# A gated linear-attention and MLP kernel, planned in source, against a written-out order in which two pairs hold neighbouring tokens together

## The chip, the cores and the metric

The kernel runs on one core of a Trainium2 chip. The metric is the time of one execution in microseconds (us) on the device, the median of several runs; lower is better. The core has five engines with queues of their own that run in order: TensorE (PE, matmuls, with weight loads shown as PEld), VectorE (DVE), ScalarE (ACT), GpSimd (POOL) and SyncE (SP, which here only issues DMAs). Where a DMA is issued from SP or POOL, it is moved by DMA engines that all queues share.

## The reference

```
f = 1 / (1 + exp(-f_logit))                        # q, k, v, f_logit: (4, 8, 768, 48) float32
for t in range(768):                               # state: 48 x 48 per batch and head
    state = f[t][:, None] * state + outer(k[t], v[t])
    y[t] = q[t] @ state
x = y as (4 * 768, 8 * 48)                         # 3072 tokens of 384
h = x @ w_in                                       # w_in (384, 2048)
out = (h * sigmoid(h)) @ w_out                     # w_out (2048, 384)
```

## The kernel before, in words

A unit is one chunk of 128 tokens of one batch with all 8 heads; there are 6 chunks x 4 batches = 24 units, and two neighbouring units (two batches of one chunk) make a pair, 12 in all. Within a unit the recurrence is done in chunk form. E and L (ScalarE) make log(1 + exp(-f_logit)). cs (PE) sums it along the tokens with a triangular matrix and gives the chunk's total with a matmul by ones. ia, a and al (ScalarE) are exponentials of those sums. ki and qg multiply them on k and q; vb casts v. tq (PE) transposes both products, eight 128x128 pieces per unit, and qkc copies them out of PSUM. sc (PE) makes the scores, at (VectorE) masks them, y (PE) multiplies by v and adds q times the state. yc casts y, yT (PE) transposes it, xc copies it to xT. d, sd and su carry the state to the next chunk of the batch. The MLP takes a pair at a time: mi (PE) makes 2 of 16 blocks of the hidden layer, six matmuls of 256 columns; si (ScalarE) applies silu; mo (PE) is a quarter of the second product for one unit, four matmuls of 384 columns; oc copies and so stores. wi and wo are four loads each of the two weights, cast to bf16 by POOL's DMA queue.

Every step is a task with an engine, a planned duration and buffers of fixed counts (SLOTS). `schedule` simulates the five queues with rank numbers from CFG, and the program emits the tasks by planned start. So the order of each engine is fixed when the program is built, and on the chip each engine waits for the next instruction of that order. PSUM's eight banks are dedicated: three to the MLP (`mlp`), two to the scores, one each to tq with yT, to cs, and to y with d. The loads take 192-byte runs, one token of one head each; the first two pairs are loaded unit by unit (192 KB per DMA), the others by pair (384 KB). An exponential table that has both exp and ln is loaded once ahead; the later table loads are put in by the compiler ahead of the activations that need one.

Of the kernel before, what the change touches and what calls it, by code (L numbers as in the profile page):

```python
# [37 lines left out]

SLOTS = dict(f=5, k=6, q=6, v=5, e=2, lf=3, ia=2, qk=5, vb=6, qkT=4, atm=3, yb=3, xT=4, hT=4, sd=2, al=6, o=3,
             st0=1, st1=1, st2=1, st3=1, mlp=3, sc=1, tq=1, cs=1, yd=1)  # L40

LAT = {"PE": 0.25, "ACT": 0.14, "DVE": 0.14, "POOL": 0.08, "SP": 0.0}
TABLE = 1.29


class Task:
    def __init__(self, name, eng, dur, prio, deps=(), acq=(), use=(), mode=None, phase=None, load=0.0):
        self.name, self.eng, self.dur, self.prio = name, eng, dur, prio
        self.deps, self.acq, self.use = list(deps), list(acq), list(use)
        self.mode, self.phase, self.load = mode, phase, load  # L50


class Inst:
    def __init__(self, key, cls):
        self.key, self.cls = key, cls


def make_tasks(cfg):
    T, tasks, pace, R = {}, [], cfg["pace"], cfg["rank"]

    def add(name, *a, **k):
        t = Task(name, *a, **k)
        T[name] = t
        tasks.append(t)
        return t

    kb = lambda n: n * 1024.0 / (cfg["dma_rate"] * 1e3)
    I = {}

    def inst(key, cls):  # L70
        if key not in I:
            I[key] = Inst(key, cls)
        return I[key]

    base = lambda u: pace * u
    for P in range(PAIRS):
        u0 = 2 * P
        for n, x in enumerate("fkqv"):
            inst((x, P), x)
        groups = [(u0,), (u0 + 1,)] if P < 2 else [(u0, u0 + 1)]  # L80
        for us in groups:
            for n, x in enumerate("fkqv"):
                add((x, us), "SP", 0.35 * len(us), base(us[0]) + R['ld'] + n * 0.1, acq=[I[x, P]], load=kb(192 * len(us)))
    load_of = lambda x, u: T[x, (u,)] if u < 4 else T[x, (u - u % 2, u - u % 2 + 1)]

    for P in range(PAIRS):
        us_list = [(2 * P,), (2 * P + 1,)] if P < 2 else [(2 * P, 2 * P + 1)]
        for us in us_list:
            n = len(us)
            ph = us[0] // 2 - 1 if us[0] >= 4 else 0  # L90
            e = add(("E", us), "ACT", 0.067 + 0.32 * n, base(us[0]) + R['E'], deps=[T["f", us]], acq=[inst(("e", us), "e")],
                    use=[I["f", P]], mode="exp", phase=ph)
            add(("L", us), "ACT", 0.067 + 0.32 * n, base(us[0]) + R['E'] + 0.1, deps=[e], acq=[inst(("lf", P), "lf")],
                use=[I["e", us]], mode="exp", phase=ph)
    log_of = lambda u: T["L", (u,)] if u < 4 else T["L", (u - u % 2, u - u % 2 + 1)]

    for u in range(UNITS):
        c, b, P, B = u // BATCHES, u % BATCHES, u // 2, base(u)
        last, ph = c == CHUNKS - 1, u // 2
        dmat = u >= cfg["turned"]  # L100
        for key in ("cs", "ia", "qk", "vb", "qkT", "atm", "yb", "sc", "al"):
            inst((key, u), key)
        inst(("y", u), "yd"), inst(("d", u), "yd"), inst(("tq", u), "tq"), inst(("yT", u), "tq")
        inst(("sd", u), "sd"), inst(("st", u), f"st{b}"), inst(("xT", P), "xT"), inst(("hT", P), "hT")
        cs = add(("cs", u), "PE", 0.162 + (0 if last else 0.1), B + R["cs"], deps=[log_of(u)], acq=[I["cs", u]], use=[I["lf", P]])
        ia = add(("ia", u), "ACT", 0.387, B + R["ia"], deps=[cs], acq=[I["ia", u]], use=[I["cs", u]], mode="exp", phase=ph)
        a = add(("a", u), "ACT", 0.38, B + R["ia"] + 0.1, deps=[ia], use=[I["cs", u]], mode="exp", phase=ph)
        if not last:
            al = add(("al", u), "ACT", 0.19, B + R["ia"] + 0.2, deps=[cs], acq=[I["al", u]], use=[I["cs", u]], mode="exp", phase=ph)
        ki = add(("ki", u), "POOL", 1.02, B + R["ki"], deps=[ia, load_of("k", u)], acq=[I["qk", u]], use=[I["ia", u], I["k", P]])  # L110
        vb = add(("vb", u), "POOL", 0.62, B + R["vb"], deps=[load_of("v", u)], acq=[I["vb", u]], use=[I["v", P]])
        qg = add(("qg", u), "DVE", 0.45, B + R["qg"], deps=[a, load_of("q", u)], acq=[I["qk", u]], use=[I["cs", u], I["q", P]])
        if dmat:
            qkT = add(("qkD", u), "SP", 2.3, B + R["tq"], deps=[qg, ki], acq=[I["qkT", u]], use=[I["qk", u]], load=0.5)
        else:
            tq = add(("tq", u), "PE", 0.45, B + R["tq"], deps=[qg, ki], acq=[I["tq", u]], use=[I["qk", u]])
            qkT = add(("qkc", u), "DVE", 0.6, B + R["qkc"], deps=[tq], acq=[I["qkT", u]], use=[I["tq", u]])
        sc = add(("sc", u), "PE", 0.41, B + R["sc"], deps=[qkT], acq=[I["sc", u]], use=[I["qkT", u]])
        at = add(("at", u), "DVE", 1.21, B + R["at"], deps=[sc], acq=[I["atm", u]], use=[I["sc", u]])
        yd = [at, vb] + ([T["su", u - BATCHES]] if c else [])  # L120
        y = add(("y", u), "PE", 0.39 if c else 0.22, B + R["y"], deps=yd, acq=[I["y", u]],
                use=[I["atm", u], I["vb", u], I["qkT", u]] + ([I["st", u - BATCHES]] if c else []))
        yc = add(("yc", u), "DVE", 0.47, B + R["yc"], deps=[y], acq=[I["yb", u]], use=[I["y", u]])
        yT = add(("yT", u), "PE", 0.17, B + R["yT"], deps=[yc], acq=[I["yT", u]], use=[I["yb", u]])
        xc = add(("xc", u), "DVE", 0.3, B + R["xc"], deps=[yT], acq=[I["xT", P]], use=[I["yT", u]])
        if not last:
            d = add(("d", u), "PE", 0.17, B + R["d"], deps=[ki, vb, y], acq=[I["d", u]], use=[I["qk", u], I["vb", u]])
            sdd = [d] + ([T["su", u - BATCHES]] if c else [])
            sd = add(("sd", u), "DVE", 0.47, B + R["sd"], deps=sdd, acq=[I["sd", u]],
                     use=[I["d", u]] + ([I["st", u - BATCHES]] if c else []))  # L130
            add(("su", u), "POOL", 0.75, B + R["su"], deps=[sd, al], acq=[I["st", u]], use=[I["sd", u], I["al", u]])

    for n in range(4):
        add(("wi", n), "POOL", 0.8, R["wi"] + n, deps=[T["ki", cfg["w_after"][n]]], load=786.432e3 / 341e3)
    for n in range(4):
        add(("wo", n), "POOL", 0.8, R["wo"] + n, deps=[T["ki", cfg["w_after"][4 + n]]], load=786.432e3 / 341e3)

    for P in range(PAIRS):
        B = base(2 * P + 1)
        for j in range(NTILES // 2):  # L140
            h = inst(("h", P, j), "mlp")
            mi = add(("mi", P, j), "PE", 0.655, B + R["mi"] + j * R["mstep"], deps=[T["xc", 2 * P], T["xc", 2 * P + 1], T["wi", j // 2]],
                     acq=[h], use=[I["xT", P]])
            add(("si", P, j), "ACT", 0.504, B + R["si"] + j * R["mstep"], deps=[mi], acq=[I["hT", P]], use=[h], mode="silu")
        for i in range(2):
            u = 2 * P + i
            o = inst(("o", u), "mlp")
            for m in range(4):
                mo = add(("mo", u, m), "PE", 0.655, B + R["mo"] + (4 * i + m) * R["mstep"],
                         deps=[T["si", P, 2 * m], T["si", P, 2 * m + 1], T["wo", m]] + ([T["mo", u, m - 1]] if m else []),  # L150
                         acq=[o], use=[I["hT", P]])
# [405 lines left out]
```

## Time and profile before

| | us |
|---|---|
| median of 3 timed runs | 221.58 (218.91 to 223.65) |
| span of the profiled execution (the results list no other time for it) | 217.2 |
| busy, PE / DVE / ACT / POOL | 181.0 / 102.7 / 149.4 / 75.0 |

The profile is one execution, from its first to its last instruction; the timed runs have launch and end around that. Busy time counts the time in which an instruction of the engine was under way, and matmuls overlap one another.

### The profile page before, as it was taken

What the parts mean: (1) busy time and instruction counts of PE and PEld (TensorE: products, weight loads), DVE (VectorE), ACT (ScalarE), POOL (GpSimd) and SP (SyncE); (2) the same over time, 40 slices, a digit from 0 to 9 for tenths busy, and PEclk for the clock granted to TensorE, in tenths of its full rate; (3) what the DMA queues carried; (4) which work ended last, traced back from release to release, by engine and by line L of the source; (5) the groups of instructions that cost most, each with busy time, mean ns of one, the idle gap of its engine ahead of it and who ended that gap; (6) DMA issues with size and microseconds to landing.
All of it is one profiled execution on the core that took longest, in us unless ns stands there. A gap on an engine that the chain in (4) does not pass through costs nothing.

```text
span 217.2 us, 4591 instructions
## 1 busy us (share of the span) xinstructions
PE 181.0 (83%) x1872; PEld 135.4 (62%) x1872; DVE 102.7 (47%) x201; ACT 149.4 (69%) x230; POOL 75.0 (35%) x126
## 2 busy tenths in 40 slices
PE   0366889945999966969969969986999999999992
PEld 0344668624578646648748738754769677786761
DVE  3277730027455526545545446444585573745111
ACT  4444249965079899995999995999845658662440
POOL 2248830042274146144343335235253321510100
PEclk9999999995699999999999999999999999999999
DMA  7999999999999999999999999011001010100101
GB/s 121 164 163 169 196 188 184 178 164 187 174 223 220 164 200 167 197 194 177 179 194 180 163 191 185 4 38 38 3 36 39 0 39 36 39 36 3 41 31 72
DMA packets 104628, 27.02 MB, mean 124 GB/s; under 512 B 99712, under 2 KB 103552, under 8 KB 104608
## 3 DMA queue, kind: packets, MB, share of 16 engines
q1 hardware_dynamic: 99488, 19.27, 70.1%
q0 software_dynamic: 5120, 7.47, 15.1%
q8 instruction: 14, 0.23, 0.5%
q14 instruction: 6, 0.05, 0.1%
HBM read 25.17 MB, written 4.72 MB: 138 GB/s over the span
## 4 chain that ended last, share of the span: by engine, by line
PE 62%; ACT 19%; DMA 6%; SPq 5%; issue 3%; DVE 2%; POOL 0%; DVEq 0%; ACTq 0%; POOLq 0%
PE mlp L412 27%; PE mlp L422 21%; SPq L381 5%; ACT L438 4%; DMA w_out_sb<-in_moe_w_out_dram 3%; PE tq L454 3%; ACT lf L390 3%; PE sc L465 3%; ACT L390 3%; DMA f<-in_f_logit_dram 2%; ACT e L388 2%; ACT L388 2%; ACT ia L438 2%; PE yd L478 2%; PE cs L431 2%
## 5 line engine op out<-in xcount | busy, mean ns | idle before, releaser
L408 ACT ACTIVATE hT<-mlp 128x512 bf16<-128x512 f32 x96 | 56.1, 597 | 28.6 <-PE mlp L412 25.0
L422 PE MATMUL mlp<-w_out_sb,hT 128*128 128x384 bf16 x384 | 71.5, 331 | 2.6 <-DMA w_out_sb<-in_moe_w_out_dram 2.6
L412 PE MATMUL mlp<-xT,w_in_sb 128*128 128x256 bf16 x576 | 68.8, 276 | 3.3 <-DVE o L425 1.7
L412 PEld LDWEIGHTS <-w_in_sb 128*128 128x128 bf16 x576 | 55.8, 99 | 11.5 <-issue 3.6
L422 PEld LDWEIGHTS <-hT 128*128 128x128 bf16 x384 | 35.6, 99 | 23.0 <-issue 3.6
L469 DVE TENSOR_TENSOR atm<-sc,triu 128x512 bf16<-128x512 f32 x48 | 30.9, 685 | 31.0 <-PE sc L465 30.9
L444 POOL TENSOR_TENSOR qk<-k,ia 128x384 bf16<-128x384 f32 x24 | 23.9, 996 | 58.5 <-ACT ia L438 50.4
L448 DVE TENSOR_TENSOR qk<-q,cs 128x384 bf16<-128x384 f32 x24 | 13.2, 550 | 37.5 <-ACT al L442 36.3
L428 POOL DMA_DIRECT2D out_dram<-o x22 | 12.7, 576 | 41.6 <-DVE o L425 36.7
L505 POOL TENSOR_TENSOR st<-sd,al 48x192 bf16<-48x192 f32 x40 | 20.0, 500 | 19.4 <-DVE sd L499 8.2
L438 ACT ACT_TABLE_LOAD x14 | 18.0, 1283 | 9.2 <-PE cs L435 8.6
L454 PE MATMUL tq<-ident,qk 128*128 128x128 bf16 x192 | 16.8, 238 | 8.9 <-DVE xT L488 6.2
L456 DVE COPY qkT<-tq 128x1024 bf16<-128x1024 bf16 x24 | 16.5, 687 | 8.5 <-PE tq L454 8.5
L425 DVE COPY o<-mlp 128x384 f32<-128x384 f32 x24 | 13.2, 552 | 15.0 <-PE mlp L422 14.9
L454 PEld LDWEIGHTS <-qk 128*128 128x128 bf16 x192 | 13.2, 106 | 11.2 <-issue 6.9
L438 ACT ACTIVATE ia<-cs 128x384 f32<-128x384 f32 x24 | 11.7, 490 | 11.6 <-PE cs L435 7.5
L431 PE MATMUL cs<-lf,triu 128*128 128x384 bf16 x24 | 8.4, 350 | 13.2 <-ACT lf L390 7.9
L482 DVE CAST yb<-yd 128x384 bf16<-128x384 f32 x24 | 13.3, 554 | 10.9 <-PE yd L478 10.7
L388 ACT ACTIVATE e<-f 128x768 f32<-128x768 f32 (+1 forms) x14 | 10.5, 748 | 8.0 <-DMA f<-in_f_logit_dram 8.0
L446 POOL CAST vb<-v 128x384 bf16<-128x384 f32 x24 | 11.7, 503 | 10.5 <-issue 5.0
L435 PEld LDWEIGHTS <-lf 128*128 128x128 bf16 x80 | 5.1, 100 | 15.1 <-issue 13.8
L408 ACT ACT_TABLE_LOAD x10 | 12.8, 1283 | 0.2
(35 smaller groups left out, 154.3 us busy)
## 6 DMA issues: line engine op xcount, KB each, us to landing
out_dram<-o POOLq DMA_DIRECT2D x22, 192.0 KB, 3.9
f<-in_f_logit_dram SPq DMA_DIRECT2D x10, 384.0 KB, 8.1
k<-in_k_dram SPq DMA_DIRECT2D x10, 384.0 KB, 7.7
q<-in_q_dram SPq DMA_DIRECT2D x10, 384.0 KB, 7.9
v<-in_v_dram SPq DMA_DIRECT2D x10, 384.0 KB, 7.8
w_in_sb<-in_moe_w_in_dram POOLq DMA_DIRECT2D x4, 384.0 KB, 9.2
w_out_sb<-in_moe_w_out_dram POOLq DMA_DIRECT2D x4, 384.0 KB, 12.0
f<-in_f_logit_dram SPq DMA_DIRECT2D x4, 192.0 KB, 5.2
```

Of the source, the lines that this page charges most:

```text
L388: nc.scalar.activation(e, at("f", u // 2)[:, i:i + n, :, 0:D], AF.Exp, scale=-1.0)
L408: return nc.scalar.activation(at("hT", P)[:, 2 * j:2 * j + 2, :], h, AF.Silu)
L412: nc.tensor.matmul(h[:, i, :], w_in_sb[:, kk, n * 128:(n + 1) * 128], at("xT", P)[:, kk, :], start=(kk == 0), stop=(kk == KT - 1))
L422: nc.tensor.matmul(o, at("hT", P)[:, n, i * C:(i + 1) * C], w_out_sb[:, n, :], start=(n == 0), stop=(n == NT - 1))
L425: nc.vector.tensor_copy(at("ob", u), at("o", u)[:, 0:d_model])
L438: nc.scalar.activation(at("ia", u).rearrange("p h d -> p (h d)"), at("cs", u)[:, 0:HD], AF.Exp)
L444: nc.gpsimd.tensor_mul(at("qk", u)[:, 1, :, 0:D], at("k", P)[:, i, :, 0:D], at("ia", u))
L454: nc.tensor.transpose(t_ps[:, j, p, :], at("qk", u)[:, j, 2 * p:2 * p + 2, :], ident)
L456: nc.vector.tensor_copy(at("qkT", u), at("tq", u).rearrange("p (j n c) -> p j n c", j=2, c=C))
L469: nc.vector.tensor_mul(at("atm", u)[:, r], at("sc", u)[:, r], triu[:, None, :].to_broadcast([C, NP, C]))
L482: nc.vector.tensor_copy(at("yb", u), at("y", u))
L505: nc.gpsimd.tensor_mul(at("st", u)[lo:lo + D, :, r * D:(r + 1) * D], at("sd", u)[lo:lo + D, :, r * D:(r + 1) * D], at("al", u)[lo:lo + D, ...
```

## The change

The planner is gone: the order of all engines, the engine of each step and its buffers are now written out in a string, PLAN, of `name.pair.index:engine:buffer`, with P, A, V, G and S for PE, ACT, DVE, POOL and SP. PAIRS says which (batch, chunk) units a pair holds. Pairs 0 and 1 are of form T: chunks 0 and 1 of batch 0, and of batch 1. In a T pair partition p holds tokens 2p and 2p + 1, so that the loads take runs of 384 bytes; index 0 or 1 is then the even or the odd token in cs, ia, ki, tq, sc and at, while y, d and what follows are again by chunk (rows 0 to 63 and 64 to 127). Pairs 2 to 11 are of form N, two batches of one chunk as before. yc, oc, vb, qkc, xc and sd may run on ScalarE now, ki and qg on VectorE or POOL. All PSUM tiles come from one pool of eight banks, pb. For pairs 0 and 1, mi is done in halves of 128 columns, one unit each. From pair 6 on, tq with qkc is replaced by a DMA transpose, qkD, and yT with xc by yD, both in SP's queue. `idle` is a number of matmuls on zeros. The k, q and v loads of N pairs go unit by unit, f by pair. Table loads are issued by the program at each turn between the exponentials and silu.

```diff
+PAIRS = [
+    ('T', (0, 0), (0, 1)),
+    ('T', (1, 0), (1, 1)),
+    ('N', (2, 0), (3, 0)),
...
+PLAN = """
+f.0.0:S:0 f.0.1:S: f.1.0:S:1 k.0.0:S:0 q.0.0:S:0 E.0.0:A:0 q.1.0:S:1 E.0.1:A: L.0.1:A:0 k.1.0:S:1 L.0.0:A: E.1.0:A:1 idle.512.17::7 cs.0.0:P:0
...
-    tasks = planned(CFG, SLOTS)
...
+            if T:
+                h = H // parts
+                w = h * 2 * D
+                src = SRC[kind][b, j * h:(j + 1) * h, c * C:(c + 2) * C].rearrange("h (p t) d -> p h (t d)", t=2)
+                dst = at(kind, P)[:, j * w:(j + 1) * w].rearrange("p (h w) -> p h w", h=h)
...
+                cols = slice(rest[2] * C, (rest[2] + 1) * C) if len(rest) > 2 else slice(0, 2 * C)
                 for kk in range(KT):
-                    nc.tensor.matmul(h[:, i, :], w_in_sb[:, kk, n * 128:(n + 1) * 128], at("xT", P)[:, kk, :],
+                    nc.tensor.matmul(h[:, i, cols], w_in_sb[:, kk, n * 128:(n + 1) * 128], at("xT", P)[:, kk, cols],
                                      start=(kk == 0), stop=(kk == KT - 1))
...
+        if kind == "y" and T:
+            first = [True, True]
+            for j in range(2):
+                for h in range(H):
+                    for r in range(2):
+                        rows = slice(r * HC, (r + 1) * HC)
+                        nc.tensor.matmul(at("y", P, r)[:, D * h:D * (h + 1)], at("atm", P, j)[rows, h % 2, h // 2, :],
+                                         at("vb", P, j)[rows, h, :], start=first[r], stop=(j == 1), skip_group_check=True)
...
         elif kind == "oc":
-            nc.vector.tensor_copy(at("ob", u), at("o", u)[:, 0:d_model])
+            copy(eng, at("ob", P, i), at("o", P, i)[:, 0:d_model])
...
+            if T:
+                for j in range(2):
+                    nc.tensor.matmul(main, tincl if j <= i else tstrict, lf[:, j, :, 0:D], start=(j == 0), stop=(j == 1), skip_group_check=True)
...
         elif kind == "qkD":
-            nc.sync.dma_start_transpose(out=at("qkT", u).rearrange("p j n c -> p (j n) c"),
-                                        in_=at("qk", u).rearrange("p j h d -> p (j h d)"))
+            nc.sync.dma_start_transpose(out=at("qkT", P, i).rearrange("p j n c -> p (j n) c"), in_=at("qk", P, i).rearrange("p j h d -> p (j h d)"))
...
+        elif kind == "yD":
+            nc.sync.dma_start_transpose(out=at("xT", P)[:, :, i * C:(i + 1) * C], in_=at("yb", P, i))
...
+    def run(kind, rest, eng, got):
+        if kind == "idle":
+            for _ in range(rest[1]):
+                nc.tensor.matmul(buf["pb", int(got)][:, 0:rest[0]], triu, zero[:, 0:rest[0]], start=True, stop=True, skip_group_check=True)
+            return
...
+    modes = [(n, mode_of(kind)) for n, (kind, *_) in enumerate(plan) if mode_of(kind)]
+    turns = {n: TABLES[m2] for (n, m), (_, m2) in zip(modes, modes[1:]) if m != m2}
...
+        for n, t in enumerate(plan):
+            if t not in loads:
+                run(*t)
+            if n in turns:
+                nc.scalar.preload_act_table_set(turns[n])
```

ScalarE, before, the exponentials of the third pair (f2, lf2; one cs bank) after the silu of the first two:

```order
L388 ACT_TABLE_LOAD
L388 ACTIVATE e0_83<-f2_63 128x768
L390 ACT_TABLE_LOAD
L390 ACTIVATE lf2_87<-e0_83 128x16x48
L438 ACT_TABLE_LOAD
L438 ACTIVATE ia0_88<-cs0_139 128x384
L440 ACTIVATE cs0_139<-cs0_139 128x384
L442 ACTIVATE al4_125<-cs0_139 128x4
L438 ACTIVATE ia1_89<-cs0_139 128x384
```

And now, the turn ahead of the exponentials of pair 3 (f3), with a copy of xT among them:

```order
L478 ACT_TABLE_LOAD
L232 ACTIVATE e1_84<-f3_64 128x768
L239 ACTIVATE lf0_85<-e1_84 128x16x48
L312 ACTIVATE al4_132<-pb2_142 128x4
L183 COPY xT2_120<-pb1_141 128x3x128
L312 ACTIVATE al5_133<-pb6_146 128x4
L310 ACTIVATE x2_90<-pb6_146 128x384
L310 ACTIVATE x3_91<-pb6_146 128x384
L310 ACTIVATE x4_92<-pb2_142 128x384
L310 ACTIVATE x1_89<-pb2_142 128x384
```

The table load behind E and the one ahead of ia are gone; one stands at the turn. In all, ScalarE's queue has 38 table loads before and 20 now.

POOL, before, from the first w_in loads to the last w_out load (st is su's result, qk4 is ki of the third pair's first unit):

```order
L400 DMA w_in_sb_144<-in_moe_w_in_dram 128x3x512 x3
L444 TENSOR_TENSOR qk3_93<-k1_67,ia1_89 128x8x48
L505 TENSOR_TENSOR st10_131<-sd1_120,al1_122 48x4x48 x2
L400 DMA w_in_sb_144<-in_moe_w_in_dram 128x3x512
L446 CAST vb3_98<-v1_79 128x384
L403 DMA w_out_sb_145<-in_moe_w_out_dram 128x4x384 x3
L505 TENSOR_TENSOR st20_132<-sd0_119,al2_123 48x4x48 x2
L505 TENSOR_TENSOR st30_133<-sd1_120,al3_124 48x4x48 x2
L444 TENSOR_TENSOR qk4_94<-k2_68,ia0_88 128x8x48
L403 DMA w_out_sb_145<-in_moe_w_out_dram 128x4x384
```

And now, what follows on one row with all four w_in loads and two casts of v (st00 and st10 are su of the T pairs, qk4 and qk1 are qg of pair 2, st30 and st20 su of its units):

```order
L386 TENSOR_TENSOR st00_148<-sd0_126,al1_129 48x4x48 x2
L386 TENSOR_TENSOR st10_149<-sd1_127,al0_128 48x4x48 x2
L386 TENSOR_TENSOR st10_149<-sd0_126,al0_128 48x4x48 x2
L386 TENSOR_TENSOR st00_148<-sd1_127,al1_129 48x4x48 x2
L208 DMA w_out_sb_162<-in_moe_w_out_dram 128x4x384
L315 TENSOR_TENSOR qk4_97<-q2_73,x4_92 128x8x48
L315 TENSOR_TENSOR qk1_94<-q2_73,x1_89 128x8x48
L208 DMA w_out_sb_162<-in_moe_w_out_dram 128x4x384
L386 TENSOR_TENSOR st30_151<-sd0_126,al3_131 48x4x48 x2
L208 DMA w_out_sb_162<-in_moe_w_out_dram 128x4x384 x2
L386 TENSOR_TENSOR st20_150<-sd1_127,al2_130 48x4x48 x2
```

The w_out loads stand behind su of the T pairs, qg and su of pair 2.

SP, before, loads of pairs (number after the letter: buffer):

```order
L381 DMA f1_62<-in_f_logit_dram 128x16x48
L381 DMA k0_66<-in_k_dram 128x16x48
L381 DMA q0_72<-in_q_dram 128x16x48
L381 DMA v1_79<-in_v_dram 128x16x48
L381 DMA f2_63<-in_f_logit_dram 128x16x48
```

And now, in the place of pairs 6 and 7:

```order
L226 DMA v1_78<-in_v_dram 128x8x48
L226 DMA k1_66<-in_k_dram 128x8x48
L330 DMA_TRANSPOSE qkT1_106<-qk3_96 128x8x128
L226 DMA f0_61<-in_f_logit_dram 128x16x48
L226 DMA v0_77<-in_v_dram 128x8x48
L226 DMA k2_67<-in_k_dram 128x8x48
L226 DMA k1_66<-in_k_dram 128x8x48
L330 DMA_TRANSPOSE qkT3_108<-qk1_94 128x8x128
L371 DMA_TRANSPOSE xT2_120<-yb0_115 128x3x128
L226 DMA f1_62<-in_f_logit_dram 128x16x48
L371 DMA_TRANSPOSE xT2_120<-yb1_116 128x3x128
L330 DMA_TRANSPOSE qkT2_107<-qk4_97 128x8x128
```

Loads stand between transposes, each of which waits for its input.

## Rows read from the trace of the kernel before

**Rows 1.** The page: busy share of each engine, and GB/s in 40 slices.

```profile
PE 181.0 (83%) x1872; PEld 135.4 (62%) x1872; DVE 102.7 (47%) x201; ACT 149.4 (69%) x230; POOL 75.0 (35%) x126
...
GB/s 121 164 163 169 196 188 184 178 164 187 174 223 220 164 200 167 197 194 177 179 194 180 163 191 185 4 38 38 3 36 39 0 39 36 39 36 3 41 31 72
```

**Rows 2.** Stretches: from:to, length, busy (count) per engine, PEclk, DMA share, GB/s.

```profile
24.35:62.30 37.95, 31.22 (x266) 22.50 (x265) 12.70 (x24) 22.37 (x34) 10.06 (x16) 0.87 1.31 186
62.30:150.00 87.70, 75.15 (x841) 57.06 (x840) 44.53 (x85) 79.62 (x115) 36.08 (x62) 1.00 1.13 160
150.00:213.46 63.46, 62.92 (x647) 47.40 (x646) 31.11 (x58) 36.46 (x60) 16.52 (x26) 1.00 0.08 29
```

**Rows 3.** The chain: start, us, piece; attention and MLP pieces of TensorE.

```profile
62.31 0.26 PE cs L431
...
65.08 0.33 PE sc L465 x8
...
65.69 0.45 PE tq L454 x8
66.14 3.29 PE mlp L412 x30
...
137.63 0.28 PE yd L474 x4
137.91 0.20 PE yd L478 x8
138.10 1.95 PE mlp L422 x12
...
142.14 0.20 PE yd L494 x4
```

**Rows 4.** The chain: w_out, and ScalarE from 72 to 147 us.

```profile
47.11 7.54 DMA w_out_sb<-in_moe_w_out_dram
...
72.22 1.28 ACT L390
...
93.04 0.84 ACT lf L390
93.90 1.28 ACT L438
95.20 0.49 ACT ia L438
...
146.35 1.28 ACT L390
```

**Rows 5.** Timeline of the first 25 us: start, us, engine, instruction [idle before].

```profile
3.96 0.52 ACT L388 ACTIVATE e<-f 128x384 f32<-128x384 f32 x1 [1.95 <-DMA f<-in_f_logit_dram]
...
16.70 1.14 SPq L381 DMA_DIRECT2D v<-in_v_dram  x1
...
23.29 11.42 SPq L381 DMA_DIRECT2D q<-in_q_dram  x1
...
24.35 1.46 PE L412 MATMUL mlp<-xT,w_in_sb 128*128 128x256 bf16 x6
```

**Rows 6.** DMA: two queues (packets, MB, share of 16 engines), and issues with KB each and us to landing.

```profile
q1 hardware_dynamic: 99488, 19.27, 70.1%
q0 software_dynamic: 5120, 7.47, 15.1%
...
q<-in_q_dram SPq DMA_DIRECT2D x10, 384.0 KB, 7.9
...
f<-in_f_logit_dram SPq DMA_DIRECT2D x4, 192.0 KB, 5.2
```

**Rows 7.** Groups by line: name, count | busy us, mean ns | idle before.

```profile
L469 DVE TENSOR_TENSOR atm<-sc,triu 128x512 bf16<-128x512 f32 x48 | 30.9, 685 | 31.0 <-PE sc L465 30.9
...
L448 DVE TENSOR_TENSOR qk<-q,cs 128x384 bf16<-128x384 f32 x24 | 13.2, 550 | 37.5 <-ACT al L442 36.3 <-ACT cs L440 1.2
...
L438 ACT ACTIVATE ia<-cs 128x384 f32<-128x384 f32 x24 | 11.7, 490 | 11.6 <-PE cs L435 7.5 <-PE cs L431 4.0
```

More of the change, by code (lines that the diff above doesn't have):

```diff
@@ L39 @@
[L39 to L50, printed above, removed]
@@ L53 @@
[L53 to L151, printed above, removed]
-            oc = add(("oc", u), "DVE", 0.47, B + R["oc"] + 4 * i, deps=[mo], acq=[inst(("ob", u), "o")], use=[o])
-            late = u >= UNITS - 2
-            add(("so", u), "SP" if late else "POOL", 0.35 if late else 0.8, B + R["so"] + 4 * i, deps=[oc], use=[I["ob", u]],
-                load=0.6)
-    return tasks, T
@@ L320 @@
+mo.11.0.3:P: oc.11.0:A:5 so.11.0:S:
+"""
 @with_exitstack
@@ L363 @@
     ones = sb.tile([C, 1], BF16, name="ones")
+    zero = sb.tile([C, 512], BF16, name="zero")
+    two = any(kind == "T" for kind, *_ in PAIRS)
+    if two:
+        tincl = sb.tile([C, C], BF16, name="tincl")
+        tstrict = sb.tile([C, C], BF16, name="tstrict")
+        halves = sb.tile([C, 2], BF16, name="halves")
+        masks = [sb.tile([C, C], BF16, name=f"mask{j}") for j in range(2)]
     w_in_sb = sb.tile([128, KT, d_ff], BF16, name="w_in_sb")
@@ L371 @@
+    where_u = {(b, c): (P, i) for P, (kind, *us) in enumerate(PAIRS) for i, (b, c) in enumerate(us)}
     where = {}
[L372 to L374 removed]
     at = lambda *key: where[key]
[L377 to L381 removed]
@@ new lines, in emit @@
+        if kind == "d" and T:
+            todo = [r for r in range(2) if us[r][1] < CHUNKS - 1]
+            for j in range(2):
+                vv = at("vb", P, j).rearrange("p (n r) d -> p n (r d)", r=2)
+                for p in range(NP):
+                    for r in todo:
+                        rows = slice(r * HC, (r + 1) * HC)
+                        d_ps = at("d", P, r)[:, 0:HD].rearrange("p (n w) -> p n w", w=2 * D)
+                        nc.tensor.matmul(d_ps[:, p, :], at("qk", P, j)[rows, 1, 2 * p:2 * p + 2, :], vv[rows, p, :],
+                                         start=(j == 0 and p == 0), stop=(j == 1), skip_group_check=True)
+            return
@@ L476, in emit @@
                     first = False
-            for h in range(H):
-                nc.tensor.matmul(y[:, D * h:D * (h + 1)], at("atm", u)[:, h % 2, h // 2, :], at("vb", u)[:, h, :],
-                                 start=first, stop=True, skip_group_check=True)
-                first = False
+            if kind == "y":
+                for h in range(H):
+                    nc.tensor.matmul(y[:, D * h:D * (h + 1)], at("atm", P, i)[:, h % 2, h // 2, :], at("vb", P, i)[:, h, :],
+                                     start=first, stop=True, skip_group_check=True)
+                    first = False
@@ L508, in emit, with takes @@
         else:
             raise ValueError(kind)
+    def takes(kind, rest):
+        if kind in ("wi", "wo", "so", "yi", "idle"):
+            return []
+        P = rest[0]
+        T = PAIRS[P][0] == "T"
+        if kind in SRC:
+            return [(kind, P)]
+        if kind in ("E", "L"):
+            return [("e" if kind == "E" else "lf", P)]
+        if kind == "mi":
+            return [("h", P, rest[1])]
+        if kind in ("si", "xc", "yD"):
+            return [("hT" if kind == "si" else "xT", P)]
+        if kind == "al":
+            return [("al", *rest)]
+        if T and kind in ("y", "d"):
+            return [(kind, P, i) for i in range(2) if kind == "y" or PAIRS[P][1 + i][1] < CHUNKS - 1]
+        if kind in ("qkc", "qkD"):
+            return [("qkT", P)] if T else [("qkT", *rest)]
+        if kind == "sc":
+            return [(f"s{r}", *rest) for r in range(2)]
+        if kind == "at":
+            return [("atm", *rest[:2])]
+        if kind == "mo":
+            return [("o", *rest[:2])]
+        return [({"ki": "qk", "qg": "qk", "yc": "yb", "oc": "ob", "su": "st"}.get(kind, kind), *rest[:2])]
@@ new lines @@
+    cls_of = lambda kind: {"e": "e", "ia": "x", "a": "x", "cs": "pb", "tq": "pb", "y": "pb", "yT": "pb", "d": "pb", "o": "pb", "s0": "pb",
+                           "s1": "pb", "h": "pb"}.get(kind, kind)
+    mode_of = lambda kind: "silu" if kind == "si" else "exp" if kind in ("E", "L", "ia", "a", "al") else None
+    TABLES = {"exp": "natural_log_exp_and_others", "silu": "silu_and_others"}
+    def run(kind, rest, eng, got):
+        if kind == "idle":
+            for _ in range(rest[1]):
+                nc.tensor.matmul(buf["pb", int(got)][:, 0:rest[0]], triu, zero[:, 0:rest[0]], start=True, stop=True, skip_group_check=True)
+            return
+        slots = iter(got.split(",") if got else [])
+        for key in takes(kind, rest):
+            if key not in where:
+                cls = cls_of(key[0])
+                if cls == "st":
+                    cls = f"st{PAIRS[key[1]][1 + key[2]][0]}"
+                elif cls == "qkT" and len(key) == 2:
+                    cls = "qkTT"
+                where[key] = buf[cls, int(next(slots))]
+        assert next(slots, None) is None, (kind, rest, got)
+        emit(kind, rest, eng)
@@ L516 @@
         make_upper_triangular(nc, triu, 1.0, diag=True)
+        nc.vector.memset(zero, 0.0)
         nc.vector.memset(ones, 1.0)
+        if two:
+            nc.gpsimd.memset(tincl, 0.0)
+            nc.gpsimd.memset(tstrict, 0.0)
+            for r in range(2):
+                half = slice(r * HC, (r + 1) * HC)
+                make_upper_triangular(nc, tincl[half, half], 1.0, diag=True)
+                make_upper_triangular(nc, tstrict[half, half], 1.0, diag=False)
+            nc.vector.memset(halves, 0.0)
+            for r in range(2):
+                nc.vector.memset(halves[r * HC:(r + 1) * HC, r:r + 1], 1.0)
@@ L523 @@
             nc.vector.memset(buf[f"st{b}", 0], 0.0)
-        for t in tasks:
-            if t not in first:
-                emit(t)
+        if two:
+            for r in range(2):
+                half = slice(r * HC, (r + 1) * HC)
+                for j in range(2):
+                    for t in range(2):
+                        nc.vector.tensor_copy(masks[j][half, t * HC:(t + 1) * HC], (tincl if j <= t else tstrict)[half, half])
+        for n, t in enumerate(plan):
+            if t not in loads:
+                run(*t)
+            if n in turns:
+                nc.scalar.preload_act_table_set(turns[n])
 _INS = ['q', 'k', 'v', 'f_logit', 'moe_w_in', 'moe_w_out']
```

488 lines of the change are left out of this document (225 added, 263 removed).

## Prediction

> **What bounds the kernel now.** I read the busy shares first, then stretches of the span, the chain that ended last, and single rows. TensorE is the busiest engine and ScalarE the next [rows 1]. The stretches say where TensorE loses time [rows 2]. Up to 24.35 us it mostly waits for the first loads and the attention steps of the first units. From 24.35, where the first MLP matmul runs, to 62.3 it is busy 31.22 of 37.95 us, at a granted clock of 0.87 on average. From 62.3 to 150 it is idle for 87.70 - 75.15 = 12.55 us, and ScalarE is busy 79.62 of the 87.70. From 150 on it is idle for half a microsecond; then 3.74 us (217.20 - 213.46) of last copy and store follow.
>
> Busy time overstates overlapping matmuls, so I price PE work by chain pieces, where one piece begins as the other ends [rows 3]: six 256-column matmuls (one mi) 3.29 / 30 x 6 = 0.66 us, four 384-column ones (one mo) 0.65, the eight transposes of tq 0.45 (three, yT: 0.17), sc 0.33, the state part of y 0.28, its other part 0.20, d 0.20, cs 0.26. All of before: 96 mi 63.2, 96 mo 62.4, tq 10.8, yT 4.1, sc 7.9, y 24 x 0.20 + 20 x 0.28 = 10.4, d 4.0, cs 6.2: 169.0 us. Ahead of 24.35 lie four cs, tq and sc, three y, two yT and d, 5.5 us. So 163.5 us of work take 213.46 - 24.35 = 189.1 us, and **25.6 us are lost**: 13.1 after 62.3 (12.55 + 0.54), 12.5 before. The 12.5 hang on the fourth w_out load: it stands in POOL's queue behind the ki of the third pair, is issued at 47.11 and lands 7.54 us later [rows 4], and the matmuls after it run at the lower level for some time.
>
> **PE work.** The change takes 12 of 24 tq and 12 of 24 yT off PE (units of pairs 6 to 11): 12 x 0.62 = 7.4 us less. It adds in the first two pairs, by matmul counts at the same prices: sc 16 instead of 8 matmuls, 4 x 0.33 = 1.3; y and yi 0.8; d 0.8; cs 0.7. The mi in halves has twice the matmuls of half the columns; tq's row (128 columns, 0.056 us each) puts that at no cost. New total 165.2. Ahead of the first mi now stand nearly all attention of the T pairs and cs of pair 2: cs 2.2, tq 1.8, sc 2.6, d 1.6, y and yi 1.9, yT 0.3 = 10.4. **Left: 154.8 us**, plus two idle matmuls of 0.2. The 31 wide idle matmuls otherwise stand where PE waits anyway; if that cover is gone they cost at most 6.7 us (31 x 0.65 / 4 x 512 / 384).
>
> **The start.** Before, the first E runs at 3.96 us, a 192-KB load is issued each 1.14 us, and the first mi comes at 24.35, at 1.46 us for six, twice the later time, so at the lower of the two levels [rows 3, 5]. A T tensor (393,000 bytes) is 1024 runs of 384 bytes instead of 2048 of 192. Packet price only: 1.14 us; byte price only: 2.28. The queues' packets lie between: those of 194 bytes on average (19.27 MB in 99488) took 0.701 x 16 x 217.2 us, 24.5 ns each, those of 1459 bytes 102 ns [rows 6]. On a straight line through both, 384 bytes take 36 ns, 1.5 times a short one, so I take 1.14 x 1.5 = 1.7. Seven T tensors (to v of pair 0) then need 12 us (8 to 16) on top of some 2 of first latency, k of pair 1 is there near 13, two ki of 1.0 us follow on POOL, and the w_in loads go out at about 15. Then the tensors behind them, f of pair 2 and v of pair 1, crawl: such a load took 11.42 us in SP's queue while weights were in flight [rows 5]. v of pair 1 feeds vb, then d.1, which stands ahead of yT.0.0 on PE. On the other side VectorE has to do eight at (0.685) and about eleven others near 0.55 between its first qg (about 10 us: 3.96, then 3.8 of E and L, cs, and three exponentials) and xc.0.0: 11.5 us, so 21.5 at best [rows 7]. **First mi at 23** (21 to 29). Both pairs then have their MLP ready at once. New masks, memsets and cumulative-sum triangles run on POOL and VectorE while the first f is in flight; without that cover about 2 us.
>
> **The weights.** The last two w_out loads now stand behind su of unit (2,1) on POOL, which needs sd, now a ScalarE copy, and that needs d.2.1 on PE, behind 12.5 us of mi, tq and sc: 23 + 12.5 + 0.5 + 1.1 = 37; at 7.54 us they land from 44.6. PE reaches the first matmul that wants them some 7 us after d.2.1, at 42.5. That is a wait of 2 to 4 us where before the whole stretch lost 12.5. **I take 4** (0 to 9). Queued behind those POOL loads is only su of (2,0), wanted much later.
>
> **ScalarE.** By the orders, 38 table loads become 20, one at each turn between exponentials and silu: each at 1.28 [rows 4], 18 x 1.28 = 23.0 us. But 35 copies come over from VectorE and POOL: 30 of 384 columns, by ia's row 0.49, and five of 1024, about 1.0: 19.7 us [rows 7]. ScalarE's volume hardly falls, by 3.3 of 149.4 us, while PE's falls by 3.8: by volume the two stand to each other as before. What does change is the chain E, L, cs, ia: before, two loads stood in it per pair (lf, load, ia at 93.04, 93.90) and a load waited behind ia's semaphore [rows 4]; the new loads are issued at the turn, ahead of the wait. Eight such loads lie on the chain from 72.22 to 146.35 (its first and last), 10.3 us beside the 12.55 lost. The copies give part back: the loss is between 3 and 13, **I take 8**, as the volumes argue for the upper half.
>
> **DMA transposes.** 12 of 256 KB (qkD) and 12 of 96 KB (yD) now run in SP's queue between loads. No row shows one. Lower bound: they land within the PE work that the order puts between them and their reader (3.3 to 8.6 us, from the prices above), cost 0. Upper: rival A. The nearest row is the 192-KB load, 5.2 us from issue to landing [rows 6], close to the median cover, 5.2: I take 0. What SP queues behind a transpose that waits for its input are loads for pairs two or more ahead. [...]
>
> **Sum.** 23 + 154.8 + 0.4 + lost 12 (4 + 8) + the end as before 3.7 = 193.9 us of span. The profiled execution of before spans 217.2; the three timed runs have a median of 221.58, 4.4 more, which I add: **198 us**, own range 192 to 205. A measurement of this kernel tells about 2% from no change (217.1 to 226).
>
> **Rivals.** *A, slower: the transposes land late.* With loads of 384 KB in SP's queue the landing was 7.9 us [rows 6]. At 8 us each, the excess over the covers is 27 us for the qkD and 25 for the later yD of each pair; the two units of a pair wait together, so about half of both, 26 us: 224. Even with before at about 7.7 us. For it: same queue, same engines, and the loads run to 136 us today (25 full slices of 5.43 us [rows 1]). Against: most of the loads ahead are done by pair 9, and the new loads are 192 KB.
> *B: as much is lost as now.* ScalarE is as full relative to PE, and a fixed order stands still wherever one step is late. 25.6 lost instead of 12: 212.
> *C: little is lost.* The turns hide in ScalarE's waits and eight shared PSUM banks replace three for the MLP: 4 lost, 190. [...]
> *D: the loads of two tokens gain nothing* (byte price) and v of pair 1 crawls behind the weights: first mi at 29, 204.
>
> **Chances.** Forecast 0.42, C 0.20, B 0.17, D 0.12, A 0.09. C reaches down to 186, B up to 214; leaving A and the ends of B and C out, the range is 188 to 214. A is split between slower 0.05 and same 0.04, and 0.02 of B reaches into same: faster 0.89, same 0.06, slower 0.05.
>
> **What the new profile would show.** Right: first mi at 21 to 25; a gap or none before the third mo of pair 0; table loads 20; PE idle 5 to 12 us between the first mo and pair 8, ScalarE over 85% busy there; sc never waiting over 1 us on a transpose. Wrong: PE waits on qkT or xT with a DMA as releaser (A); long waits on cs behind lf (B); the v load of pair 1 landing after 24 (D). An error in the start moves the end one for one, since PE is packed behind it.

## The result, and the profile after

The changed kernel takes **187.48 us** (186.34 to 188.51, 4 runs) beside 221.28 before (218.91 to 223.65): ratio 0.851, interval 0.843 to 0.859. That is 33.8 us less, where I forecast 23.6; the time lies 0.5 us below the low end of my range. In a later session the same kernel had 186.38 (185.31 to 188.00). Of the kernel with short runs (experiment 4) only the lowest of four runs is compared, as the others took over 1.5% longer.

The page of the kernel after: busy shares, granted clock and GB/s in 40 slices, and one group (busy us, mean ns).

```profile
span 186.2 us, 4811 instructions
...
PE 175.7 (94%) x1953; PEld 129.1 (69%) x1953; DVE 84.3 (45%) x173; ACT 134.0 (72%) x243; POOL 61.2 (33%) x106
...
PEclk9997599999999999999999999999999999999999
...
GB/s 131 297 281 208 191 197 161 216 162 179 211 161 224 196 212 211 88 52 170 119 198 93 160 179 191 98 230 162 186 159 225 104 167 200 193 61 65 189 130 85
...
L315 DVE TENSOR_TENSOR qk<-q,x 128x384 bf16<-128x384 f32 x18 | 12.4, 703 | 11.0 <-ACT x L310 8.3
```

TensorE is busy 94% of the span instead of 83% [rows 1], and in the second to fourth slice the loads run at 208 to 297 GB/s instead of 163 to 169. The stretches, cut at the first mi (24.46), at 62.3 and 150 as before, and at TensorE's last matmul:

```profile
24.46:62.30 37.84, 36.99 (x487) 29.56 (x482) 17.82 (x35) 28.53 (x52) 9.95 (x16) 1.00 1.06 190
62.30:150.00 87.70, 85.68 (x931) 63.72 (x929) 41.63 (x77) 76.87 (x138) 33.39 (x51) 1.00 0.80 159
150.00:182.86 32.86, 32.84 (x280) 24.17 (x277) 9.58 (x18) 13.99 (x27) 5.54 (x9) 1.00 0.56 136
```

TensorE is idle for 0.85 us in the first of these (6.73 before) and for 2.02 in the second (12.55 before) [rows 2]. Its waits (us in total, times, longest) name what is left; the first two rows stand ahead of the first mi, and all waits behind it come to 2.7 us:

```profile
PE pb L339 <- ACT qkTT L183: 1.3, 1, 1.3
PE pb L427 <- DVE qkTT L185: 1.2, 1, 1.2
...
PE pb L282 <- DMA w_out_sb<-in_moe_w_out_dram: 0.8, 2, 0.5
PE pb L343 <- DMA qkT<-qk: 0.8, 1, 0.8
PE pb L247 <- ACT ob L183: 0.7, 1, 0.7
```

The chain of the kernel after holds one table load of the 20, and the last w_out load:

```profile
26.04 1.28 ACT L478
...
39.35 6.29 DMA w_out_sb<-in_moe_w_out_dram
```

The DMA view has the transposes (count, median us to landing), which no row of before could show:

```profile
qkT<-qk SPq DMA_TRANSPOSE x12, 3.8
...
xT<-yb SPq DMA_TRANSPOSE x12, 2.4
```

### The profile page after: what moved, and what is told of

The parts are those of the page before. It is cut to its first block, busy times and chain, and to the rows that moved or that the text cites. A ratio compares the mean times of both kernels' runs of the same rounds, so it can differ in the third digit from the quotient of the medians.

```text
span 186.2 us, 4811 instructions
## 1 busy us (share of the span) xinstructions
PE 175.7 (94%) x1953; PEld 129.1 (69%) x1953; DVE 84.3 (45%) x173; ACT 134.0 (72%) x243; POOL 61.2 (33%) x106
## 4 chain that ended last, share of the span: by engine, by line
PE 71%; DMA 12%; ACT 8%; DVE 5%; issue 2%; POOL 1%; DVEq 0%; ACTq 0%; POOLq 0%
PE pb L282 27%; PE pb L247 26%; DMA w_out_sb<-in_moe_w_out_dram 7%; PE pb L427 4%; DVE qk L315 3%; DMA qkT<-qk 3%; PE pb L343 2%; ACT hT L252 2%; DMA out_dram<-ob 2%; PE pb L322 2%; ACT x L310 2%; PE pb L359 2%; PE pb L305 2%; PE pb L355 2%; PE pb L376 1%
## 5 line engine op out<-in xcount | busy, mean ns | idle before, releaser
L282 PE MATMUL pb<-w_out_sb,hT 128*128 128x384 bf16 x384 | 71.9, 326 | 0.9 <-DMA w_out_sb<-in_moe_w_out_dram 0.8
L252 ACT ACTIVATE hT<-pb 128x512 bf16<-128x512 f32 x96 | 52.2, 609 | 27.2 <-PE pb L247 26.8
L247 PE MATMUL pb<-xT,w_in_sb 128*128 128x256 bf16 (+1 forms) x672 | 70.3, 257 | 0.8 <-ACT ob L183 0.7
L347 DVE TENSOR_TENSOR atm<-pb,triu 128x512 bf16<-128x512 f32 x40 | 25.8, 684 | 30.3 <-PE pb L343 19.0
L478 ACT ACT_TABLE_LOAD x19 | 24.4, 1283 | 0.3
L310 ACT ACTIVATE x<-pb 128x384 f32<-128x384 f32 x48 | 21.3, 507 | 1.8 <-PE pb L305 0.8
L315 POOL TENSOR_TENSOR qk<-k,x 128x384 bf16<-128x384 f32 x15 | 15.5, 1042 | 15.8 <-DMA k<-in_k_dram 9.6
L315 DVE TENSOR_TENSOR qk<-q,x 128x384 bf16<-128x384 f32 x18 | 12.4, 703 | 11.0 <-ACT x L310 8.3
L185 DVE COPY ob<-pb 128x384 f32<-128x384 f32 x15 | 8.0, 552 | 16.2 <-PE pb L282 13.5
L380 DVE TENSOR_TENSOR sd<-pb,st 128x384 f32<-128x384 f32 x16 | 8.8, 551 | 11.4 <-PE pb L305 5.9
L427 PE MATMUL pb<-zero,triu 128*128 128x512 bf16 (+1 forms) x33 | 11.1, 481 | 2.6 <-POOL triu masks.py:66 1.4
```

The costliest lines, as they stand in the source:

```text
L185: ENG[eng].tensor_copy(dst, src)
L247: nc.tensor.matmul(h[:, i, cols], w_in_sb[:, kk, n * 128:(n + 1) * 128], at("xT", P)[:, kk, cols], start=(kk == 0), stop=(kk == KT - 1))
L252: return nc.scalar.activation(at("hT", P)[:, 2 * j:2 * j + 2, :], at("h", P, j).rearrange("p (n c) -> p n c", n=2), AF.Silu)
L282: nc.tensor.matmul(o, at("hT", P)[:, n, i * C:(i + 1) * C], w_out_sb[:, n, :], start=(n == 0), stop=(n == NT - 1))
L310: nc.scalar.activation(at(kind, P, i).rearrange("p h d -> p (h d)"), at("cs", P, i)[:, 0:HD], AF.Exp, scale=1.0 if kind == "ia" else -1.0)
L315: ENG[eng].tensor_mul(at("qk", P, i)[:, j, :, 0:D], heads("qk"[j], P, i), at("ia" if j else "a", P, i))
```

## The experiments

**1. Table loads, taken from both sides.** The changed kernel without its turn loads, and the kernel before with them:

```diff
-            if n in turns:
-                nc.scalar.preload_act_table_set(turns[n])
```
```diff
+        modes = [(n, t.mode) for n, t in enumerate(tasks) if t.mode]
+        sets = {"exp": "natural_log_exp_and_others", "silu": "silu_and_others"}
+        turns = {n: sets[m2] for (n, m), (_, m2) in zip(modes, modes[1:]) if m != m2}
...
+            if n in turns:
+                nc.scalar.preload_act_table_set(turns[n])
```

> The changed kernel without the table loads that its program issues at each turn between exp and silu, so that the compiler places them: 37 table loads stand in ScalarE's order instead of 20, and every other instruction stays where it is. Table theory: most of what the kernel before lost between 62 and 150 us came from its 38 loads, which stand on ScalarE behind waits in the exponential phases; 17 more of 1.28 us are 21.8 us on an engine that is busy 76.9 of 87.7 us in that stretch, so ScalarE becomes the later of the two there and the time rises by 6 to 15 us, to 194 to 202. Rival, the order and the eight shared PSUM banks absorb them: ScalarE waits for TensorE for 26.8 us in the changed kernel, the loads fall into these waits, and the time rises by 3 us or less.

> The kernel before with nothing changed but the table loads: its program issues one right behind the last activation ahead of each turn, 20 loads instead of 38, and its order and PSUM buffers stay. Table theory: 18 loads of 1.28 us leave ScalarE, 23.0 us, and the time falls by 6 to 13 us, to 208 to 215. Rival, order and banks: the three PSUM buffers of the MLP and the planned order set the waits, ScalarE waits longer instead, and the time stays within 3 us of 221.

Measured: 204.52 us (203.55 to 205.19) and 202.29 (201.44 to 202.81; ratio to before 0.912, 0.905 to 0.919). So 17 loads cost 17.0 us in the one kernel and 18 cost 18.8 in the other. The rival falls; the table theory is right about the cause, but both steps are larger than the 15 and 13 us that it allowed. The middle stretch of the changed kernel without turn loads, then of the kernel before with them:

```profile
62.30:150.00 87.70, 75.66 (x763) 54.97 (x763) 33.51 (x62) 79.90 (x130) 26.51 (x41) 0.96 0.67 127
```
```profile
24.35:62.30 37.95, 33.20 (x308) 24.45 (x307) 14.54 (x28) 20.05 (x35) 13.46 (x22) 0.91 1.28 194
62.30:150.00 87.70, 87.70 (x1004) 67.73 (x1002) 53.83 (x102) 70.65 (x117) 39.46 (x67) 1.00 1.11 161
```

With the compiler's loads TensorE is busy 75.66 us under the new order and was 75.15 under the old [rows 2]; with turn loads it is 85.68 and 87.70. Neither order nor banks make this difference. The chain of the changed kernel without turn loads shows how loads come to stand between TensorE's steps with their whole 1.28 us:

```profile
81.41 0.39 ACT x L310
...
81.82 1.28 ACT L239
83.12 0.84 ACT lf L239
83.98 1.28 ACT L310
85.27 0.50 ACT x L310
85.81 0.61 PE pb L322 x8
```

A load (the rows with no tile) stands ahead of lf and another ahead of the exponential behind it, and TensorE's next step follows on the second. 19 of the 37 loads are such pieces of that chain, 24.3 us; of the 20 in the changed kernel one is. The 24.3 us aren't the cost: without these loads other work would take part of their place in the chain, and the measured difference is 17.0.

**2. DMA transposes.** All 24 turned back into PE transposes with a copy on VectorE (qkD to tq and qkc, yD to yT and xc). In the first kernel the next TensorE step often wants the transpose's PSUM bank at once; the second takes banks that are wanted two or three TensorE steps later, and moves some of the transposes in the order for it. Some entries of PLAN, from the second:

```diff
-qkD.9.0:S:3
+tq.9.0:P:6
+qkc.9.0:V:3
...
-yD.7.1:S:
+yT.7.1:P:7
+xc.7.1:V:
```

> The changed kernel with the 24 DMA transposes of pairs 6 to 11 turned back into transposes on TensorE with a copy on VectorE, two to nine TensorE steps behind their inputs, in PSUM banks that are free there. Theory that TensorE's work alone sets the end: 12 of 0.45 and 12 of 0.17 us come back, 7.4 us, on an engine that is busy 57.98 of 60 us between 90 and 150, and the time rises by as much, to 193 to 197. Rival, ScalarE or the waits set the end there and TensorE's work fits in between: 2 us or less.

> Again the changed kernel with its 24 DMA transposes turned back into TensorE's transposes and copies on VectorE, this time with each in a PSUM bank that the next tenant wants only two or three TensorE steps later. With the banks handed on at once 205.6 us were measured, 7.0 us of them TensorE's added work and the rest waits of 0.4 to 0.9 us for the copies. Theory that the added work sets the end: 193 to 197 us. Rival, eight banks are too few for transposes in this order, and the waits come back elsewhere: 199 us or more.

Measured: 205.61 us (205.35 to 206.17) and 194.72 (193.81 to 195.82). The second is the one to read: 7.2 us over the changed kernel, for 7.4 of added work by [rows 3], as its theory said. The first adds 10.9 more, which neither of its two theories allowed. Both kernels have the same steps; they differ in the banks and places of the transposes. TensorE's waits for the copies behind transposes, between 62 us and the end, come to 11.0 us in the first and 0.6 in the second. The longest of the first:

```profile
PE pb L255 <- DVE qkT L193: 4.0, 5, 0.9
PE pb L313 <- DVE qkT L193: 2.2, 3, 0.8
PE pb L290 <- DVE qkT L193: 1.7, 2, 0.8
```

mi, cs and mo (L255, L313, L290) take over the bank of a transpose whose copy isn't done: up to 0.9 us each time.

**3. The fourth w_out load.** The kernel before with this load issued right behind the third, alone and with turn loads:

```diff
+    late = next(t for t in tasks if t.name == ("wo", 3))
+    tasks.remove(late)
+    tasks.insert(1 + next(n for n, t in enumerate(tasks) if t.name == ("wo", 2)), late)
```

> The kernel before with the fourth load of w_out issued right behind the third, some 20 us earlier, and every other instruction where it was. Theory that this load's place cost the kernel before most of its early loss: its own wait of 2.56 us goes, and with it the low granted clock behind it; the time falls by 3 to 6 us. Rival, the table loads set the pace there: what TensorE doesn't wait for at the weights it waits for at the first cs of the next exponential phase; the time stays within 1.5 us of 221.

> The kernel before with both edits, one table load at each turn and the early fourth load of w_out. With the table loads alone 202.3 us were measured, and TensorE still waits 1.98 us for w_out there. If the two causes are apart, that wait goes and the time is 199.5 to 201 us; if the early load takes bandwidth from the loads of the next units, the time stays at 202 or rises to 204.

Measured: 216.92 us (216.23 to 217.93; ratio 0.985, 0.977 to 0.993), and 202.72 (201.97 to 204.48) against 202.29 with turn loads alone. In both the wait for w_out is gone, but it is worth 4.1 us in the one, which is not large beside the spread of the kernel before (single runs of 214.9 to 223.9 over the sessions), and nothing in the other. Stretches of the kernel with turn loads, then of that with both edits:

```profile
46.00:50.00 4.00, 2.69 (x40) 1.86 (x38) 3.58 (x6) 2.56 (x5) 1.90 (x3) 0.75 1.47 178
50.00:54.00 4.00, 2.04 (x9) 1.17 (x10) 1.84 (x3) 0.00 (x0) 0.00 (x0) 0.50 1.19 196
54.00:58.00 4.00, 4.00 (x40) 2.52 (x38) 2.63 (x6) 1.05 (x3) 2.46 (x4) 0.90 1.38 211
```
```profile
46.00:50.00 4.00, 2.55 (x37) 1.84 (x35) 2.68 (x5) 1.33 (x5) 2.75 (x4) 0.96 1.48 167
50.00:54.00 4.00, 3.63 (x28) 2.03 (x26) 3.30 (x6) 1.69 (x2) 0.11 (x1) 0.50 1.46 166
54.00:58.00 4.00, 4.00 (x35) 2.46 (x34) 2.17 (x5) 1.05 (x3) 1.80 (x3) 0.69 1.27 218
```

The granted clock is at 0.50 from 50 to 54 with the wait and without it. Ahead of it, from 46 to 50, TensorE is busy 2.69 of 4 us (2.55 without the wait), between the attention steps of the third pair. Where the wait is gone, work lies in the slow stretch instead of idleness; the stretch begins and ends later (0.96 instead of 0.75 from 46 to 50, 0.69 instead of 0.90 from 54 to 58) and, by an estimate from these means that takes the clock to be at 0.50 or at 1.00, is as long, some 7 us. In the kernel before, the early load did shorten it, by the same estimate from 10.2 to 6.9 us (means of 46 to 62 us). The last four microseconds of the kernel before, then with the early load alone:

```profile
54.00:58.00 4.00, 3.31 (x16) 1.92 (x16) 0.80 (x2) 0.00 (x0) 0.61 (x1) 0.50 1.47 180
```
```profile
54.00:58.00 4.00, 4.00 (x37) 2.56 (x36) 2.38 (x6) 1.34 (x2) 1.18 (x2) 0.78 1.48 178
```

The 202 us that the second expectation gave to a loss of bandwidth were measured, but that profile lists no wait of TensorE for a DMA; why the slow stretch got shorter in the one kernel and not in the other is open.

**4. The loads of two tokens.** The changed kernel with each load of the first two pairs cut in two transfers: by token, with runs of 192 bytes, or by heads, with runs of 384:

```diff
-                src = SRC[kind][b, j * h:(j + 1) * h, c * C:(c + 2) * C].rearrange("h (p t) d -> p h (t d)", t=2)
-                dst = at(kind, P)[:, j * w:(j + 1) * w].rearrange("p (h w) -> p h w", h=h)
+                src = SRC[kind][b, j * h:(j + 1) * h, c * C:(c + 2) * C].rearrange("h (p t) d -> t p h d", t=2)
+                dst = at(kind, P)[:, j * w:(j + 1) * w].rearrange("p (h t d) -> t p h d", h=h, t=2)
+                for t in range(2):
+                    nc.sync.dma_start(out=dst[t], in_=src[t])
```
```diff
+                for t in range(2):
+                    g = slice(t * h // 2, (t + 1) * h // 2)
+                    nc.sync.dma_start(out=dst[:, g], in_=src[:, g])
```

> The changed kernel with the loads of its first two pairs of units cut to runs of 192 bytes: each is two transfers, one for each of the two tokens of a partition, into the same places, so that 8 of SyncE's loads of these pairs become twice as many and everything behind them is the same. Theory that the long runs set the start: the early slices fall from 297 toward the 164 GB/s of the kernel before, the first mi comes about 4 us later than 24.46, and the end with it, at 190 to 193 us. Rival, the start is set by the chain over VectorE and the copies, and the loads are early enough either way: first mi and end within 1.5 us.

> The changed kernel with each load of its first two pairs issued as two transfers of half the heads each, with the long runs of 384 bytes kept. With two transfers and runs of 192 bytes 192.7 to 199.1 us were measured: the last v loads were issued at 14.36 to 16.97, behind the start of the w_in loads, and landed at 27.5, so that y waited 5.96 us. Theory that SyncE's issue time decides this race: the same number of issues gives the same delay, and the time is 191 us or more. Rival, the length of the runs: with them the loads land as before, and the time stays within 2 us of 187.5.

Measured: 196.48 us (192.71 to 199.10; the lowest is 5.2 us over the changed kernel), and 187.51 (186.90 to 187.80), 1.1 over it in the same session and within its spread. The number of issues is not it, the length of the runs is. The profile with short runs is that of a run of 196.81 us, so its late first mi overstates what the 5.2 us hold. SyncE's rows with short runs and with long ones (start, us, transfers):

```profile
11.60 1.79 SPq L222 DMA_DIRECT2D v<-in_v_dram  x2
...
14.36 2.61 SPq L222 DMA_DIRECT2D v<-in_v_dram  x2
...
27.52 0.95 POOL L185 CAST vb<-v 128x384 bf16<-128x384 f32 x2 [8.70 <-DMA v<-in_v_dram]
```
```profile
8.96 1.14 SPq L223 DMA_DIRECT2D v<-in_v_dram  x2
...
10.70 3.13 SPq L223 DMA_DIRECT2D v<-in_v_dram  x2
```

Two halves of a v take 1.79 us of SyncE with short runs and 1.14 with long ones. The second v is then issued at 14.36 to 16.97 rather than 10.70 to 13.83, and POOL issues w_in from 15.56 (14.16 with long runs). Behind that start the v crawls: 8.70 us of wait on POOL, 5.96 on PE, the first mi at 33.1 (4 us late was expected, 8.6 came in this run).

**5. Idle matmuls.** None; 11 instead of 17 at the start and none ahead of yi.0.1; and the same with five in the gap from 13.4 to 14.7 us. The last, as entries cut out of PLAN:

```diff
-idle.512.17::7
+idle.512.11::7
...
-idle.128.2::5
+idle.512.5::0
...
-idle.512.3::3
 yi.0.1:P:
```

> The changed kernel without its idle matmuls, which compute nothing that is read. Clock theory: they hold TensorE's granted clock up in the start (0.86 on the mean of the first 24.46 us), without them the pieces ahead of the first mi run at the lower level and the time rises by 2 to 4 us. Rival, they stand in the way: the first cs has its input at 5.87 and starts at 7.7 behind idle matmuls, and those ahead of the state part of y take 1.39 us on the chain; without them the time falls by 1.5 to 3 us.

> The changed kernel with 11 idle matmuls instead of 17 at the start and none ahead of the state part of y. Theory that these stand in the way: the first cs starts 1.2 to 1.6 us earlier and the chain loses 1.39 us behind y, the time falls by 1.5 to 3 us, to 184.5 to 186. Without any idle matmul 186.3 us were measured, with the granted clock at 0.50 from about 19 to 25 us. Rival, the start is set by something beside TensorE, and the time stays within 0.7 us of the changed kernel.

> The kernel with 11 idle matmuls at the start and none ahead of the state part of y, and in place of two short idle matmuls that wait for a copy, five long ones in a free PSUM bank, so that they fill the gap from 13.4 to 14.7 us. Theory that this gap lets the granted clock fall to 0.50 at 17 us: it stays at 1.00, 2 to 3 us of work at half the clock are saved, and the time is 183 to 184.5 us. Rival, the gap from 17.2 to 18.4 us, which no free bank can fill, or a lower limit on the work ahead of it lets it fall all the same: the time is that of the kernel with fewer idle matmuls, within 0.7 us.

> The changed kernel once more, as it is, beside the other kernels of this call: 187.5 us. In its profile TensorE's granted clock stood at 0.50 from about 17 to 23 us; in two kernels with the same start, one with the compiler's table loads and one with transposes on TensorE, it stayed at 1.00. If that differs from run to run, times 2 us apart are to be expected.

Measured: 186.26 us (185.84 to 187.27), and in one session 186.54 (184.85 to 186.78), 185.36 (184.71 to 185.96) and, for the kernel unchanged, 186.38. They lie apart from one another by less than their spread, so idle matmuls neither gain nor cost a measurable time, and none of the theories of a gain or a loss holds; whether the third is better by 1.0 us stays open. The first mi comes at 22.5, 22.8, 22.6 and 22.96 us, and the granted clock falls in all of them (means of 0.50 to 0.78 from 17 to 20 us, 0.50 to 0.81 from 20 to 24). Stretches of the third:

```profile
17.00:20.00 3.00, 2.16 (x80) 1.79 (x81) 3.00 (x6) 1.98 (x5) 2.05 (x5) 0.77 1.14 172
20.00:24.00 4.00, 3.06 (x67) 2.23 (x62) 2.83 (x7) 3.05 (x9) 1.01 (x2) 0.75 1.20 184
```

Filling that gap didn't hold the clock; the theory of the gap falls. The start gives little back by now: in the third an mi then waits 0.82 us for w_in, up to 23.95.

The unchanged start differs from run to run, as the last expectation supposed. From 17 to 20 us, and at the first mi, the profile of the changed kernel, then that of the kernel with the compiler's table loads, whose order differs in table loads alone:

```profile
17.00:20.00 3.00, 1.74 (x70) 1.54 (x64) 2.74 (x5) 2.17 (x4) 1.78 (x4) 0.50 1.14 177
...
24.46 1.67 PE L247 MATMUL pb<-xT,w_in_sb 128*128 128x128 bf16 x24
```
```profile
17.00:20.00 3.00, 2.31 (x86) 1.81 (x86) 3.00 (x6) 2.17 (x5) 1.88 (x4) 1.00 1.22 201
...
21.53 0.50 PE L247 MATMUL pb<-xT,w_in_sb 128*128 128x128 bf16 x6
```

The first kernel of experiment 2 kept 1.00 as well, in each microsecond from 14 to 27. Six runs of the unchanged kernel took 185.31 to 188.00 us. What lets the clock fall in one run and not in another is not shown.

## Why the prediction was right in its direction and too high

Where the 33.8 us come from, by the runs: 17 to 19 from the table loads, 7.2 from the transposes. Some 8 to 10 are left for the rest together, and no run takes these apart. The kernel before with turn loads does TensorE's work after 62.3 without a gap, so by the traces they lie ahead of it: 0.85 us idle instead of 4.75 between the first mi and 62.3, no low clock there, and more attention done before the first mi. (Behind 62.3 the changed kernel loses 2.0 us that the other doesn't.) The long runs of the loads are part of it: without them the changed kernel takes 5.2 us more (experiment 4).

- *ScalarE, "I take 8, as the volumes argue for the upper half": this step failed.* The stretch lost 2.02. I had found the loads on the chain (eight, 10.3 of 12.55 us) and then let the volumes outvote the chain. The copies did come over as priced (20.0 us for 19.7), and ScalarE is busy 76.87 of 87.70 us, but what had held TensorE was 1.28 us between a step's input and its output, again at each of lf and ia. 70.65 or 76.87 us of volume fit beside it. The volume itself was off too: ScalarE's busy time fell from 149.4 to 134.0 us, by 15.4 where the prediction has 3.3. Rival C, at 190 us and a chance of 0.20, was nearest: "The turns hide in ScalarE's waits". Its banks are not needed for it: the kernel before has three buffers for the MLP and with turn loads loses nothing there either. The sign that failed with this step is "PE idle 5 to 12 us between the first mo and pair 8": from the first mi to the end TensorE was idle for 2.9.
- *The weights, "I take 4": 0.85.* The load came at 39.35, later than the 37 taken, and landed at 45.64; TensorE had other work until then and waited 0.8 us in two pieces. The clock stayed at 1.00. That the 12.5 us of before "hang on the fourth w_out load" holds for a third of them at most: moving it gave 4.1 us, or none.
- *The start, 23: measured 24.46, and 22.96 in another run.* The time is near; the price of the loads in it is not. The straight line through two packet prices has 1.7 us for a T tensor and 12 for seven; a v with long runs takes 1.15 us of SyncE (two halves with short ones 1.79), and all seven were issued by 8.64 us, as by the packet price alone (8). k of pair 1 was there at 11.28 instead of 13, and the w_in loads went out at 13.55 instead of 15. On the other side VectorE took longer than its price in the profile of after: two qg ahead of the first mi took 1.35 us each instead of 0.55 (last section). In the run with 22.96 neither did. The prediction takes the 1.46 us of the first mi of before for the lower clock level (0.50 in that profile from 50 to 58 us) by their length; the profile's granted clock reads 1.00 there (24 to 28 us), so the two rows disagree, and no run settles it.
- *PE work left, 154.8 + 0.4:* busy 155.51. *Transposes, 0:* one wait of 0.8 us for the twelve of q and k, none for the twelve of y. They land in 3.8 and 2.4 us at the median, where rival A took 8.
- *The end, 3.7 + 4.4: 3.35 + 1.3.* The 4.4 put the median of three runs beside the span of one. The profiled run of after took 187.92 us for a span of 186.2, so 1.7 is what launch and end cost; the other 2.7 were the difference between runs of before (221.58 is the median, 218.91 the run that fits a span of 217.2).

Of the 10.8 us between the sum (198.3) and the time, the losses make 9.1 (12 taken, 158.40 - 155.51 = 2.9 measured) and the end 3.5; the start and PE's work take 1.8 back.

A table load takes 1283 ns on the mean in the profiles of before and after alike. In the chain of experiment 1 the activation behind a load starts 0.01 to 0.02 us after its end (83.10 to 83.12), and 17 loads cost 17.0 us, 1.0 each.

## What to carry to other kernels

Count table loads by their place: here each one ahead of a step of a serial chain cost about 1.0 us of the end, and those at a turn between phases hardly any (one of 20 on the chain), whatever the engine's busy share said. When the chain and the volumes of a profile disagree on what a loss is made of, test the chain first; here it was right. A wait that is taken out of a stretch at the lower clock (0.50 here) may give nothing, as it did in one of two kernels here; look at the clock of the stretch before you price the wait.
